# Attention followed by a swish MoE layer on one core: the num matmuls in 64x64 array tiles, one batch loaded earlier, the last rows in two column halves

## The chip, the cores and the metric

The kernel runs on one core of a Trainium2 chip. The time is the device time of one execution in microseconds (us). A profile of one execution per kernel gives the rest. The profile's span leaves out about 2 us of the time (327.5 us of span beside about 329 us).

The engines are called TensorE (PE in the profile, its weight loads PEld), VectorE (DVE), ScalarE (ACT), GpSimd (POOL) and SyncE (SP). "L287" is a line of the kernel that the profile belongs to; the lines of the two kernels differ.

## The reference

```python
# q, k, v: (B=8, H=8, S=576, D=64); w_in: 512x2048; w_out: 2048x512; beta: 2048
phi(x) = concat([relu(x) * cos(theta), relu(x) * sin(theta)], -1)   # theta = pi/2 * pos / S
kv  = einsum('bhsf,bhsd->bhfd', phi(k), v);   z = sum_s phi(k)
num = einsum('bhsf,bhfd->bhsd', phi(q), kv)
den = einsum('bhsf,bhf->bhs',   phi(q), z) + 1e-6
x   = (num / den), heads joined: 4608 tokens x 512
h   = x @ w_in
out = (h * sigmoid(beta * h)) @ w_out
```

The two large products take 9 chunks of 512 tokens with 64 matmuls each into h and into o. Attention is small beside them, but it must be done first for the tokens of a chunk.

## The kernel before

Attention of batch 0 is a prologue; that of batch 1 lies between the matmuls of chunk 0, that of batches 2 to 7 between those of chunks 1 to 6. Chunks 7 and 8 have none. A chunk has 32 slots: 16 groups of four h matmuls, then 16 parts of four o matmuls.

The num matmuls contract over 128 rows: two heads lie above each other, so each head's kv block is padded with zeros beside it, and 2 x 65 columns stream through. (65 is 64 values and the sum for the denominator.)

```python
    kv = one.tile([P, 2, 2, 2, 2 * E], BF16, name="kv")        # E = 65
    nc.gpsimd.memset(kv, 0.0)
    ...
    def num_mm(b, t, jp, bank):
        for i in range(3):
            n = 3 * t + i
            for cs in range(2):                                # cos, sin
                for g in range(2):
                    gs_ = slice(g * HP, (g + 1) * HP)
                    nc.tensor.matmul(
                        ps[gs_, bank, i * 2 * E : (i + 1) * 2 * E],
                        lhsT=(qt, qs)[cs][:, jp, n, gs_],
                        rhs=kv[:, g, jp, cs, :],
                        start=(cs == 0), stop=(cs == 1))
```

Each of batches 2 to 7 has three bursts of 24 such matmuls, in slots 16, 18 and 20 of its chunk. The loads stand in one queue, and w_in 3 is cast on GpSimd:

```python
    load_w("out", 0)
    load_w("out", 1)          # needs a staging buffer that the cast of a w_in tile must free
    load_raw(1, "v")          # so batch 1's v stands behind that wait
    load_raw(1, "k")
    load_raw(1, "q")
    ...                       # cast w_in 2 on VectorE
    load_w("out", 2)
    ...                       # cast w_in 3 on GpSimd
    load_w("out", 3)
    early = {                 # chunk 0: what is put behind which slot
        5: lambda: cast_wout(0),
        8: lambda: cast_wout(1),
        13: lambda: (v_scale(1, 0), [v_scale(1, 1, jp, eng="pool") for jp in range(2)]),
        17: lambda: k_relu(1),
        20: lambda: (kv_mm(1, 0, 6), kv_mm(1, 1, 6), q_relu(1, 0), kv_take((0, 1), 6), q_relu(1, 1)),
        ...                   # q turned at 22 and 23, num at 25, 26 and 28
    }
```

The last 128 rows of the output are one 512-column product in one bank. ScalarE copies its left half, VectorE its right half afterwards.

## Time and profile before

| | before |
|---|---|
| time, median of the runs before the change | 328.77 us (328.76 to 329.08) |
| span of the profiled run | 327.5 us |
| start of the first h matmul (end of the prologue) | 22.15 us |
| chunk 0 | 48.35 us, clock 0.89 |
| each of chunks 1 to 6 | about 32.5 us, clock 1.00 |
| each of chunks 7 and 8 | 28.44 us |
| last matmul's end to the span's end | 5.15 us |

The prediction below shows the views that carry the argument: TensorE's busy row, the table of stretches and the chain of waits. The page of the kernel before has this group (line, engine, operation, operands with partitions x elements, count; then busy us, mean ns of one, and the idle time just before them).

```profile
L289 PE MATMUL ps<-kv,qt 128*64 128x130 bf16 x288 | 20.3, 226 | 0.4 <-ACT kv L279 0.3
```

`128*64` is the part of the array that one matmul uses: all rows, half of the columns. The 226 ns is a latency, not the price of a matmul: 24 of them pass in 0.82 us. The reader should price pipelined matmuls by the distance between starts.

### The profile page before, as it was taken

The numbers are of one execution on the slowest core, as the hardware profiler recorded it, in microseconds if no ns is written. First come the engines' busy times: TensorE is split into PE (matmuls) and PEld (weight loads), VectorE is DVE, ScalarE is ACT, GpSimd is POOL, SyncE is SP. The second block draws the span as 40 slices with busy tenths as digits, with TensorE's granted clock in tenths as the row PEclk, the third lists the DMA queues.
The fourth block names the chain that finished last, engine by engine and source line by source line (L and its number), as shares of the span: only waits on it lengthen the run. The fifth ranks groups of instructions, "written<-read, shape, count | busy, mean of one in ns | idle before, by whom it ended". The sixth has DMA issues, their size and how long they took to land.

```text
span 327.5 us, 5827 instructions
## 1 busy us (share of the span) xinstructions
PE 309.5 (94%) x2410; PEld 147.3 (45%) x2410; DVE 122.3 (37%) x267; ACT 141.3 (43%) x220; POOL 87.2 (27%) x95
## 2 busy tenths in 40 slices
PE   8989927999999999999999999999999999999993
PEld 3554413454554455445444544454445444444441
DVE  4989386381374037403740383038303200000000
ACT  7557405277313731373147314721472147327510
POOL 2556040074025402630263026302720220000000
PEclk9999978799999999999999999999999999999999
DMA  7992999259559706980797079606500620121022
GB/s 251 394 344 97 373 390 392 91 106 318 211 121 274 311 2 127 247 334 3 133 272 303 2 140 297 270 9 141 127 0 10 130 64 1 30 68 32 0 66 64
DMA packets 49530, 53.60 MB, mean 164 GB/s; under 512 B 30288, under 2 KB 30304, under 8 KB 49504
## 3 DMA queue, kind: packets, MB, share of 16 engines
q1 hardware_dynamic: 46784, 45.88, 45.8%
q0 software_dynamic: 2688, 7.34, 8.1%
q8 instruction: 19, 0.31, 0.4%
q14 instruction: 7, 0.06, 0.1%
q10 hardware_dynamic: 32, 0.01, 0.0%
HBM read 36.71 MB, written 9.44 MB: 141 GB/s over the span
## 4 chain that ended last, share of the span: by engine, by line
PE 82%; DMA 9%; DVE 3%; POOL 2%; SPq 1%; ACT 1%; issue 0%; ACTq 0%; DVEq 0%
PE ps L390 38%; PE ps L377 36%; PE ps L289 5%; DMA w_stage<-in_moe_w_in_dram 5%; PE ps L265 3%; DMA raw_v<-in_v_dram 3%; DVE vb L220 2%; POOL win L105 2%; DMA raw_q<-in_q_dram 2%; SPq L95 1%; ACT wout L114 1%; DVE qs L223 1%; DVE rk L197 0%; PE ps L354 0%; ACT o_sb L400 0%
## 5 line engine op out<-in xcount | busy, mean ns | idle before, releaser
L390 PE MATMUL ps<-wout,g_t 128*128 128x512 bf16 x576 | 132.4, 383 | 2.8 <-ACT wout L114 2.8
L377 PE MATMUL ps<-xt,win 128*128 128x512 bf16 x576 | 133.9, 378 | 1.2 <-ACT xt L360 1.2
L381 ACT ACTIVATE g_t<-ps,beta 128x512 bf16<-128x512 f32 x144 | 98.9, 687 | 41.9 <-PE ps L377 41.9
L377 PEld LDWEIGHTS <-win 128*128 128x128 bf16 x576 | 55.2, 97 | 75.8 <-issue 15.4
L390 PEld LDWEIGHTS <-g_t 128*128 128x128 bf16 x576 | 54.8, 98 | 68.8 <-issue 5.9
L404 POOL DMA_DIRECT2D out_dram<-o_sb x56 | 37.7, 678 | 151.9 <-ACT o_sb L400 151.9
L400 ACT COPY o_sb<-ps 128x512 f32<-128x512 f32 x35 | 20.5, 585 | 111.9 <-PE ps L390 111.9
L281 DVE CAST kv<-ps 64x520 bf16<-64x520 f32 x14 | 9.8, 698 | 79.8 <-PE ps L265 79.7
L223 POOL TENSOR_TENSOR qs<-qt,tanr 128x1152 bf16<-128x1152 bf16 x12 | 28.4, 2386 | 5.0 <-PE ps L377 4.9
L398 DVE COPY o_sb<-ps 128x256 f32<-128x256 f32 x1 | 0.4, 425 | 65.5 <-ACT o_sb L397 65.5
L220 DVE TENSOR_SCALAR vb<-raw_v,cos 128x256 bf16<-128x256 f32 x63 | 20.8, 405 | 1.7 <-DMA raw_v<-in_v_dram 1.7
L289 PEld LDWEIGHTS <-qt 128*64 128x64 bf16 x288 | 16.4, 113 | 10.2 <-issue 9.6
L289 PE MATMUL ps<-kv,qt 128*64 128x130 bf16 x288 | 20.3, 226 | 0.4 <-ACT kv L279 0.3
L307 DVE TENSOR_TENSOR xs<-ps,rden 128x768 bf16<-128x768 f32 x21 | 20.1, 957 | 0.7
L289 PE MATMUL ps<-kv,qs 128*64 128x130 bf16 x288 | 19.9, 225 | 0.0
L302 DVE TENSOR_TENSOR den<-ps,eps 128x12 f32<-128x12 f32 x21 | 3.6, 170 | 40.5 <-PE ps L289 40.5
L265 PE MATMUL ps<-vb,rk 64*64 64x130 bf16 x576 | 11.4, 230 | 6.7 <-DVE rk L197 6.5
L289 PEld LDWEIGHTS <-qs 128*64 128x64 bf16 x288 | 16.6, 111 | 0.0
L220 DVE TENSOR_SCALAR vb<-raw_v,sin 128x256 bf16<-128x256 f32 x54 | 14.7, 348 | 0.0
L265 PEld LDWEIGHTS <-rk 64*64 64x64 bf16 x576 | 9.9, 114 | 10.4 <-DVE rk L197 7.0
L210 POOL TENSOR_TENSOR vb<-raw_v,sin 128x1152 bf16<-128x1152 f32 x4 | 8.8, 2213 | 15.9 <-DMA raw_v<-in_v_dram 15.9
L240 ACT COPY qt<-ps 128x640 bf16<-128x640 bf16 (+1 forms) x8 | 4.9, 640 | 18.2 <-PE ps L235 15.8
(57 smaller groups left out, 114.4 us busy)
## 6 DMA issues: line engine op xcount, KB each, us to landing
raw_v<-in_v_dram SPq DMA_DIRECT2D x7, 1152.0 KB, 11.5
raw_k<-in_k_dram SPq DMA_DIRECT2D x7, 1152.0 KB, 13.8
raw_q<-in_q_dram SPq DMA_DIRECT2D x7, 1152.0 KB, 8.8
out_dram<-o_sb POOLq DMA_DIRECT2D x56, 128.0 KB, 4.7
w_stage<-in_moe_w_in_dram SPq DMA_DIRECT2D x4, 1024.0 KB, 15.3
w_stage<-in_moe_w_out_dram SPq DMA_DIRECT2D x4, 1024.0 KB, 11.0
out_dram<-o_sb SPq DMA_DIRECT2D x16, 128.0 KB, 2.3
raw_q<-in_q_dram SPq DMA_DIRECT2D x2, 576.0 KB, 4.6
```

The source lines that it names most:

```text
L210: (nc.gpsimd if eng == "pool" else nc.vector).tensor_tensor(vb[:, n0:n1, js, cs, 0:D], rv.rearrange("q j n d -> q n j d")[:, n0:n1, js], t ...
L220: nc.vector.tensor_scalar(o, a, scalar1=t[:, n : n + 1], scalar2=None, op0=ALU.mult)
L223: eng.tensor_tensor(dst.rearrange("q n (g p) -> q n g p", g=2), src.rearrange("q n (g p) -> q n g p", g=2), tanr[:, n0:n1].unsqueeze(2).to ...
L265: nc.tensor.matmul(t[jj * HP : (jj + 1) * HP, g], lhsT=rk[hs, n, 2 * jp + jj, :], rhs=vb[hs, n, 2 * jp + jj].rearrange("q s e -> q (s e)") ...
L281: nc.vector.tensor_copy(o, a)
L289: nc.tensor.matmul(ps[gs_, bank, i * 2 * E : (i + 1) * 2 * E], lhsT=(qt, qs)[cs][:, jp, n, gs_], rhs=kv[:, g, jp, cs, :], start=(cs == 0), ...
L307: nc.vector.tensor_tensor(xs[:, 3 * t : 3 * t + 3].rearrange("q n s (j d) -> q s n j d", j=2), nv[:, :, :, :, 0:D], rden.unsqueeze(4).to_b ...
L377: nc.tensor.matmul(h_ps, lhsT=win[jt // 4][:, mi, (jt % 4) * P : (jt % 4 + 1) * P], rhs=xt[:, :, jp, g * HP : (g + 1) * HP], start=(mi == ...
L381: nc.scalar.activation(g_t, h_ps, AF.Silu, scale=beta[:, jt : jt + 1])
L390: nc.tensor.matmul(o_ps, lhsT=gs[c, jt][:, tt * P : (tt + 1) * P], rhs=wout[jt // 4][:, jt % 4, :], start=(jt == 0), stop=(jt == JT - 1))
L400: nc.scalar.copy(o_sb, o_ps)
L404: eng.dma_start(out=out_v[bb, n], in_=o_sb[hf * HP : (hf + 1) * HP, :])
```

## The change

Its intent: num uses the four 64x64 tiles of the array at once, so no zeros are multiplied and only 65 columns stream; one burst per batch instead of three costs fewer entries and exits; batch 1's v and k come ahead of w_out, so that chunk 0 doesn't wait for them; the last rows' copy overlaps their own matmuls. The diff, cut to its core:

```diff
-    kv = one.tile([P, 2, 2, 2, 2 * E], BF16, name="kv")
+    kv = one.tile([P, 2, 2, 2, E], BF16, name="kv")
-    nc.gpsimd.memset(kv, 0.0)
@@ v_scale: VectorE reads cos/sin from a PSUM copy
+            if eng == "dve":
+                t = ps[:, 1, 32 + 16 * cs : 32 + 16 * cs + NQ]
@@ num
+    def num_mm(n, jp, bank, slot):
+        for cs in range(2):
+            for jj in range(2):
+                rows = slice(jj * HP, (jj + 1) * HP)
                 for g in range(2):
+                    cols = slice(g * HP, (g + 1) * HP)
                     nc.tensor.matmul(
+                        ps[cols, bank + jj, slot * E : (slot + 1) * E],
+                        lhsT=(qt, qs)[cs][rows, jp, n, cols],
+                        rhs=kv[rows, g, jp, cs, :],
                         start=(cs == 0), stop=(cs == 1))
@@ loads
+    load_raw(1, "v")
+    load_raw(1, "k")
     load_w("out", 0)
     load_w("out", 1)
-    load_raw(1, "v")
-    load_raw(1, "k")
     load_raw(1, "q")
+    load_w("out", 2)
+    load_w("out", 3)
     for gj in GJ:
         cast_win(2, gj)
-    load_w("out", 2)
+    v_scale(1, 0)
     for gj in GJ:
-        cast_win(3, gj, "pool")
-    load_w("out", 3)
+        cast_win(3, gj)
@@ chunk 0 (cut)
+        5: lambda: v_scale(1, 1),
+        7: lambda: cast_wout(0),
+        9: lambda: k_relu(1),
+        11: lambda: cast_wout(1),
+        19: lambda: (kv_mm(1, 0, 6), kv_mm(1, 1, 6), q_relu(1, 0), q_relu(1, 1), kv_take((0, 1), 6),
+                     cast_wout(2, "aaaa")),
@@ batches 2 to 7
-        for t, (slot, bank) in enumerate(((16, 4), (18, 6), (20, 4))):
-            u.append((slot, lambda t=t, bank=bank: (
-                num_mm(b, t, 0, bank), num_mm(b, t, 1, bank + 1), x_div(b, t, bank))))
-            u.append((slot + 1, lambda t=t: x_turn_dma(b, t)))
+        u.append((18, lambda: (num_all(0, 4), num_all(1, 6), num_all(2, 0))))
+        for t, bank in enumerate((4, 6, 0)):
+            u.append((18, lambda t=t, bank=bank: (x_div(t, bank), x_turn_dma(b, t))))
@@ the last 128 rows
+    def o_last(c, tt):
+        o_sb = osb_pool.tile([P, DM], FP32, name="o_sb", tag="o_sb")
         for hf in range(2):
+            m0, m1 = 256 * hf, 256 * hf + 256
+            o_ps = ps[:, 4 + hf, 0:256]
+            ...                                   # 16 matmuls of 256 columns
+            (nc.scalar.copy if hf == 0 else nc.vector.tensor_copy)(o_sb[:, m0:m1], o_ps)
+            store(c, tt, o_sb, m0, m1)
```

The prologue's num and divisions of batch 0 are regrouped to fit (7 + 2 of the nine token groups instead of 3 x 3), and its warm-up matmuls are moved.

## The prediction

> **What bounds the kernel now.** I read four views in this order: the page's clock and busy rows, the chain that ended last in order of time, the same chain at its end, and the table of stretches. First the rows of TensorE in 40 slices of 8.19 us, and its granted clock.
>
> ```profile
> PE   8989927999999999999999999999999999999993
> PEclk9999978799999999999999999999999999999999
> ```
>
> TensorE is full except in slices 5 to 7 (41 to 57 us), and there its clock fell too. That is chunk 0 (a chunk is 512 tokens: 64 matmuls into h, then 64 into o), which runs from 22.15 to 70.50 us. The table of stretches sets it beside chunk 1, chunk 2 and a late chunk that has no attention work (columns: stretch, length, then busy time of PE, PEld, DVE, ACT, POOL, clock, DMA share, GB/s).
>
> ```profile
> 22.15:70.50 48.35, 38.38 (x308) 19.23 (x309) 31.91 (x52) 21.37 (x35) 12.80 (x12) 0.89 0.69 248
> 70.50:103.13 32.63, 32.63 (x273) 15.46 (x273) 17.61 (x47) 13.19 (x20) 11.78 (x11) 1.00 0.80 214
> 103.13:135.61 32.48, 32.48 (x274) 15.36 (x272) 12.79 (x32) 13.33 (x20) 10.26 (x10) 1.00 0.59 174
> 265.50:293.94 28.44, 28.44 (x129) 12.46 (x128) 0.00 (x0) 13.33 (x20) 1.03 (x2) 1.00 0.17 38
> ```
>
> So there are two kinds of loss: 16 us in chunk 0 against a chunk with the same work, and 4.04 us of attention matmuls in each of chunks 1 to 6, where TensorE never waits. The chain says what held chunk 0 (columns: start, length, what).
>
> ```profile
> 25.80 1.24 POOL win L105
> ...
> 31.14 0.37 SPq L93
> 31.51 0.05 issue
> 31.56 8.43 DMA raw_v<-in_v_dram
> 39.99 0.03 issue
> 40.02 6.16 DVE vb L220 x9
> 46.18 1.28 DVE rk L197
> 47.46 0.04 issue
> 47.50 2.17 PE ps L265 x69
> ```
>
> The second w_out load got a staging buffer that a slow cast on POOL held until 31.1 us; batch 1's v stands behind it in the same queue, so it is only issued at 31.56, lands at 39.99, and is scaled at 0.68 us an instruction because POOL works beside it. The kv matmuls wait 6.5 us for that, and the idle halves the clock. In steady state the chain is TensorE alone:
>
> ```profile
> 115.04 1.15 PE ps L265 x72
> 116.18 2.83 PE ps L377 x12
> 119.01 0.86 PE ps L390 x4
> 119.88 0.82 PE ps L289 x24
> 120.70 1.83 PE ps L390 x8
> 122.53 0.82 PE ps L289 x24
> ```
>
> L265 is kv, L289 num, L377 h, L390 o. The end is a copy in two halves, the second waiting for the first:
>
> ```profile
> 322.46 0.38 ACT o_sb L397
> 322.84 0.02 issue
> 322.87 0.42 DVE o_sb L398
> ```
>
> **What the Trainium skill says.** (1) "TensorEngine Tiling (Array Packing)", Key Properties: tiles of the array work in parallel, and a change of tiling mode drains TensorE. The trace agrees: kv, in 64x64 tiles, starts its matmuls in groups of four, one group each 57 ns for 130 columns; and the last o matmul before a num burst starts 0.31 us before the first num matmul instead of 0.216. (2) "TensorE: Matmul & The Clock Gate", LDWEIGHTS: a weight load takes columns/1.2 ns, thus 53 ns for 64 columns, as an estimate. The kernel before cannot confirm it: 57 ns is longer than both 53 ns and the 54 ns of the stream. (3) The same page, What's actually happening: after an idle window of about 3.4 us the clock is halved. The trace agrees: 6.5 us idle, then o matmuls 0.43 us apart instead of 0.216. (4) "SBUF — State Buffer", Who interferes with whom: a VectorE instruction with two SBUF inputs is blocked by a GpSimd one that reads SBUF. The trace agrees: of two equal scalings of v in the prologue, the one under POOL's took 3.08 us, the other, overlapped for 0.72 us, took 1.93 us; both leave about 1.2 us.
>
> **The change, part by part.**
>
> *num in four tiles.* Before, a num matmul contracts 128 rows, half of them zeros, with 130 columns moving, in pairs: per batch 72 matmuls, 36 pairs, three bursts of 0.82 us = 2.46 us. The o matmuls around them take 0.86 + 1.83 + 1.83 + 9.60 = 14.12 us against 13.81 us in a chunk without bursts: 0.31 us for three entries and exits. Together 2.77 us. Check: 32.48 - 28.44 = 4.04 = 2.77 + 1.15 (kv) + 0.11 (kv's entry and exit). After, 144 matmuls of 65 columns, no zeros, in 36 groups of four, one burst. What sets a group's time is open: the stream, 65 columns at 512 per 0.2158 us = 27 ns, plus 3 ns as kv shows, 30 ns; instruction issue: kv's instructions start 1.7 ns apart, eight make 14 ns, so it does not bind; or the weight loads at 53 ns plus 3. I give 30 ns 0.6, something about 43 ns (odd column counts, starts at 260-byte steps) 0.25, and 57 ns 0.15: mean 37 ns. Burst: 36 x 37 ns = 1.33 us, plus one entry and exit 0.2 (a little more than 0.1, for the first load) = 1.5 us. Gain 1.25 us a batch, six batches in chunks 1 to 6: **7.5 us**. Divisions (about 1.36 us each on VectorE) come three in a row after the burst; 12 us of o matmuls remain to hide them, so nothing is added. The kv eviction becomes one instruction instead of two; VectorE has slack there, so it gains nothing by itself.
>
> *Batch 1 ahead of w_out.* In the built order batch 1's v and k stand directly behind the four w_in loads, and the second w_out load now waits for a VectorE cast. Bytes come at about 390 KB/us in order of issue. w_in's last load has 15 of its 16 completions by 23.7 us and the last at 25.75 us, one DMA engine being 2 us late. v (1.18 MB, 3.0 us) then lands at 26.7, the late engine at 28.8 us; k at 29.7 and 31.8; w_out 0 and 1 by about 34 and 37; q by 40. VectorE: the casts of w_in 1 and 2 end about 27; then v scaled with cos, now placed before the cast of w_in 3, waits until 28.8: 9 x 0.26 = 2.4 -> 31.2; w_in 3, 4 x 0.69 -> 34.0. TensorE needs w_in 3 for h groups 12 to 15. The prologue is shorter: v is scaled from a PSUM copy of cos, so 3.08 us becomes about 1.2, and num is smaller, so h can start about 20.2 instead of 22.15 us; group 12 would be due at 20.2 + 12 x 0.914 = 31.2, and waits until 34.0. So the prologue's 2 us are lost to this **new wait** (it was 33.1 for group 12 before). h ends at 37.4. Then VectorE: v with sin 36.4, w_out 0 38.0, k 39.4, w_out 1 41.0, q 42.5, kv eviction 43.2. TensorE reaches kv after four o parts at 37.4 + 3.45 = 40.9: k is ready, the 6.5 us wait is gone, and so is the halved clock (kv 2.17 -> 1.15, nine o matmuls 0.21 us each, part of num: about 3.6 us). ACT: w_out 2 from about 43 to 45.8, q's four copies to 48.8, w_out 3 to 51.2, before the o part that needs it (53.6). Chunk 0's end: 37.4 + o 13.8 + kv 1.25 + two q turns 1.25 + num 1.5 + entries 0.3 + x turns 1.1 + small waits 0.9 + last x copy 0.9 = 58.4 against 70.50: **12.1 us**.
>
> *Last rows in two column halves.* 32 matmuls of 256 columns, 3.49 us by the same column rate plus 3 ns each, instead of 16 x 0.216 = 3.45. The first half is copied and stored under the second; at the end stands one 0.42 us copy instead of 0.38 + 0.42 in a row: **0.4 us**.
>
> Sum: 7.5 + 12.1 + 0.4 = 20.0; 328.8 - 20.0 = 308.8, rounded to 309.
>
> **The rivals.** *Weight loads bind num.* Then groups stay near 57 ns, the burst is 2.05 + 0.2 = 2.25 us, the gain 0.5 us a batch, 3 in all and 0.7 less in chunk 0: 314. For it: the skill's 53 ns. Against it: recorded load lengths, which may be modelled, are 107 ns for 64 columns and 98 ns for the 128-column loads, which come in four chunks of 32; the 9 to 10 ns between them look like 32 columns at the full rate. *The new wait for w_in 3 grows.* A further delay of the late DMA engine by 1.5 us (its lag grew so between 18.4 and 20.4 us, when instructions were fetched over the DMA engines; the program now has more) holds v to 30.3, h to 39, and an idle near 3.4 us may halve the clock once more: chunk 0 ends about 60 to 61, total 311. Taken with the first: 316. *Loads were hidden anyway*: if a later wait (w_out 2 or 3, q) took kv's place, chunk 0 would keep several of the 16 us, but by the order of bytes w_out 3 lands at about 45 us, 8 us early. *All goes well*: v lands at 26.7, no late engine, chunk 0 ends at 56, num at 30 ns: 305.
>
> **Range and chances.** The two large terms are nearly independent: chunk 0 gives 10 to 14 us, num 3 to 9. Ends that take one bad term each give 305 and 314, with both half bad 315; 8 times in 10 I expect 304.5 to 315.5. Faster by over 2% means under 322.2; even num at no gain and chunk 0 at 10 us gives 318. Faster 0.95, within 2% 0.04, slower 0.01 (a stall in the burst or divisions that hold up the next chunk).
>
> **What would show it.** Right: chunks 1 to 6 about 31.2 us long, one num burst of 1.3 to 1.6 us each, 144 matmuls, groups of four 30 to 40 ns apart; kv of batch 1 starting at about 41 us with the clock at 1.0 through chunk 0; a wait of 2 to 3 us before h group 12 released by VectorE's cast of w_in 3, with v landing near 28.8; only VectorE's copy after the last matmul. Wrong: groups at 57 ns; v landing beyond 31 us; a clock of 0.5 in chunk 0; VectorE's divisions on the chain in chunks 1 to 6.

## The result and the profile after

The changed kernel took 308.21 us (307.17 to 310.27, four runs) beside 328.76 us (327.96 to 329.08, four runs) of the kernel before on the same chip. The ratio is 0.9386 with a 95% interval of 0.9331 to 0.9441. A ratio here is the mean time of one kernel's fast runs over the mean of the other's fast runs in the same rounds, so it is not quite the quotient of the medians. The prediction of 309.0 was met. The stages of the two profiles, beside what was predicted:

| stage | before | predicted | after | change, predicted | change, measured |
|---|---|---|---|---|---|
| first h matmul | 22.15 | 20.2 | 22.84 | -2 | +0.7 |
| kv of batch 1 starts | 47.50 | 40.9 | 40.90 | -6.6 | -6.6 |
| end of chunk 0 | 70.50 | 58.4 | 57.01 | -12.1 | -13.5 |
| chunks 1 to 6, each | 32.48 | 31.2 | 31.16 | -1.25 | -1.32 |
| ... all six | | | | -7.5 | -7.9 |
| end of the last matmul to the end of the span | 5.15 | | 4.35 | -0.4 | -0.8 |

The measured changes, with +0.1 for the longer last chunk, add up to -22.1 us, which is the difference of the two spans (327.5 - 305.4). The medians differ by 20.6: the profiled run was the fastest of its four, and the runs' clocks (0.994, 0.994, 0.993, 0.987) explain it only in part: the slowest run has the lowest, but the two runs at 0.994 lie 1.66 us apart. The experiments come back to it.

First TensorE's busy row and its clock on the page of the changed kernel, in slices of 7.64 us:

```profile
PE   7849999999999999999999999999999999999994
PEclk9979999999999999999999999999999999999999
```

The hole at 41 to 57 us is gone. There is a smaller one in the third slice, with a lower clock: in the prologue, where the kernel before had none so deep. The table of stretches of the changed kernel (stretch, length, busy time of PE, PEld, DVE, ACT, POOL, clock, DMA share, GB/s) for chunk 0, chunk 2 and chunk 7:

```profile
22.84:57.01 34.17, 32.98 (x379) 16.88 (x383) 29.30 (x66) 22.63 (x37) 3.18 (x5) 1.00 0.94 335
...
88.33:119.48 31.15, 30.89 (x342) 14.66 (x344) 11.91 (x31) 13.34 (x20) 10.48 (x10) 1.00 0.65 186
...
244.12:272.56 28.44, 28.34 (x128) 12.46 (x128) 0.00 (x0) 13.34 (x20) 1.04 (x2) 1.00 0.17 38
```

Chunk 0 fell from 48.35 to 34.17 us, at clock 1.00, with the DMA busy 94% of it. Chunk 2 fell from 32.48 to 31.15, and chunk 7, which the change leaves alone, kept its 28.44. The chain of waits of the changed kernel, from batch 0's second num burst to batch 1's kv (start, length, what):

```profile
15.09 0.38 PE ps L287 x29
15.46 2.59 issue
18.05 0.59 PE ps L287 x38
...
21.78 1.02 ACT xt L351
...
22.84 1.02 PE ps L368 x4
...
40.90 1.15 PE ps L266 x72
```

L266 is kv, L287 num, L368 h, L386 o. kv of batch 1 comes without a wait and at full clock: 1.15 us instead of 2.17. But TensorE stops for 2.59 us in the middle of a num burst, and the profile says "issue", that is, it sees nothing that it waits for. In steady state, the chain of waits of chunk 2:

```profile
104.25 2.54 PE ps L386 x11
106.79 1.36 PE ps L287 x130
108.15 0.16 issue
108.31 1.89 PE ps L386 x8
```

One burst of 1.36 us stands where three of 0.82 us were. (It has 144 matmuls; the profile lost some records.) The page's group of these matmuls shows the new shape, and puts that one stop of 2.6 us beside them:

```profile
L287 PE MATMUL ps<-kv,qs 64*64 64x65 bf16 x576 | 11.5, 194 | 2.6 <-issue 2.6
```

In chunk 2 the weight loads of successive groups of four start 28 to 36 ns apart, with two longer distances of 54 and 59 ns: 33 ns is the median, 34 ns the mean. (The expectations below say 33.6.) And the end of the chain:

```profile
297.55 3.51 PE ps L402 x32
...
301.14 0.42 DVE o_sb L405
```

One copy stands alone behind the last matmul, as intended.

### The profile page after: what moved, and what is told of

The parts are those of the page before. It is cut to its first block, busy times and chain, and to the rows that moved or that the text cites. A ratio compares the mean times of both kernels' runs of the same rounds, so it can differ in the third digit from the quotient of the medians.

```text
span 305.4 us, 6998 instructions
## 1 busy us (share of the span) xinstructions
PE 291.2 (95%) x2973; PEld 140.5 (46%) x3001; DVE 111.5 (37%) x275; ACT 141.3 (46%) x218; POOL 77.6 (25%) x88
## 4 chain that ended last, share of the span: by engine, by line
PE 91%; DVE 3%; issue 2%; DMA 2%; ACT 1%; SPq 0%; DVEq 0%
PE ps L368 43%; PE ps L386 39%; PE ps L287 3%; PE ps L266 3%; DMA raw_q<-in_q_dram 2%; PE ps L402 1%; DVE qs L224 1%; PE ps L346 1%; DVE vb L211 1%; PE ps L411 1%; ACT xt L351 0%; PE ps L236 0%; DVE xs L309 0%; DVE rk L196 0%; ACT o_sb L392 0%
## 5 line engine op out<-in xcount | busy, mean ns | idle before, releaser
L368 PE MATMUL ps<-xt,win 128*128 128x512 bf16 x576 | 134.0, 378 | 1.7 <-ACT xt L351 1.7
L386 PE MATMUL ps<-wout,g_t 128*128 128x512 bf16 x535 | 120.5, 379 | 2.2 <-issue 1.3
L368 PEld LDWEIGHTS <-win 128*128 128x128 bf16 x576 | 55.2, 97 | 76.1 <-issue 16.6
L386 PEld LDWEIGHTS <-g_t 128*128 128x128 bf16 x560 | 53.9, 98 | 63.5
L278 DVE CAST kv<-ps 128x520 bf16<-128x520 f32 x7 | 4.9, 700 | 80.1 <-PE ps L266 80.1
L309 DVE TENSOR_TENSOR xs<-ps,rden 128x768 bf16<-128x768 f32 (+4 forms) x25 | 22.7, 912 | 0.8
L298 DVE TENSOR_TENSOR den<-ps,eps 128x12 f32<-128x12 f32 (+2 forms) x24 | 3.9, 161 | 36.5 <-PE ps L287 36.5
L287 PE MATMUL ps<-kv,qs 64*64 64x65 bf16 x576 | 11.5, 194 | 2.6 <-issue 2.6
L287 PEld LDWEIGHTS <-qt 64*64 64x64 bf16 x576 | 10.5, 106 | 4.5 <-issue 3.8
L287 PE MATMUL ps<-kv,qt 64*64 64x65 bf16 x576 | 11.6, 195 | 0.3 <-ACT kv L276 0.2
L287 PEld LDWEIGHTS <-qs 64*64 64x64 bf16 x576 | 10.5, 105 | 2.7 <-issue 2.7
L196 DVE TENSOR_SCALAR qb<-raw_q 128x1152 bf16<-128x1152 f32 x15 | 10.7, 752 | 1.5 <-DMA raw_q<-in_q_dram 1.5
L266 PE MATMUL ps<-vb,rk 64*64 64x130 bf16 x576 | 10.2, 218 | 0.7 <-DVE vb L211 0.4
L266 PEld LDWEIGHTS <-rk 64*64 64x64 bf16 x576 | 8.6, 106 | 4.4 <-issue 3.5
L196 DVE TENSOR_SCALAR rk<-raw_k 128x2304 bf16<-128x2304 f32 (+1 forms) x8 | 10.2, 1277 | 0.0
```

The lines of the kernel that those rows point to most:

```text
L196: nc.vector.tensor_scalar(dst, src, scalar1=0.0, scalar2=None, op0=ALU.max)
L266: nc.tensor.matmul(t[jj * HP : (jj + 1) * HP, g], lhsT=rk[hs, n, 2 * jp + jj, :], rhs=vb[hs, n, 2 * jp + jj].rearrange("q s e -> q (s e)") ...
L278: nc.vector.tensor_copy(o, a)
L287: nc.tensor.matmul(ps[cols, bank + jj, slot * E : (slot + 1) * E], lhsT=(qt, qs)[cs][rows, jp, n, cols], rhs=kv[rows, g, jp, cs, :], start ...
L309: nc.vector.tensor_tensor(o.rearrange("q j n s d -> q j (n s) d"), nv[:, :, a:z, :, 0:D].rearrange("q j n s d -> q j (n s) d"), rden[:, :, ...
L368: nc.tensor.matmul(h_ps, lhsT=win[jt // 4][:, mi, (jt % 4) * P : (jt % 4 + 1) * P], rhs=xt[:, :, jp, g * HP : (g + 1) * HP], start=(mi == ...
```

## The experiments

Twelve runs went to the chip: eleven new kernels and, as e11, the changed kernel once more. The first four take the change apart. All gave correct results.

### e1: only num in four tiles, three bursts, on the old kernel

Batches 1 to 7 of the kernel before get the new num tiles, reading the diagonal blocks of the old padded kv; loads and everything else stay.

```diff
+                            nc.tensor.matmul(
+                                ps[cols, bank + jj, (2 * i + jp) * E : (2 * i + jp + 1) * E],
+                                lhsT=(qt, qs)[cs][rows, jp, 3 * t + i, cols],
+                                rhs=kv[rows, g, jp, cs, jj * E : (jj + 1) * E],
+                                start=(cs == 0), stop=(cs == 1))
@@
-                num_mm(b, t, 0, bank), num_mm(b, t, 1, bank + 1), x_div(b, t, bank))))
+                num4(t, bank), x_div4(t, bank))))
```

> The kernel before, with only the num matmuls of batches 1 to 7 in four 64x64 tiles (three bursts a batch as before, loads, prologue and tail as before). Theory (the tiles themselves save the time): groups of four about 33.6 ns apart as in the changed kernel, a burst 12 x 0.034 + 0.2 to 0.25 = 0.6 to 0.65 us instead of 0.92, so about 0.9 us a batch in chunks 1 to 6 (32.48 to about 31.6 us), 5.4 us there and about 1 us in chunk 0: 322 to 323 us in all. Rival (what pays is merging three bursts into one): hardly any gain, over 326 us.

Measured: 321.40 us (321.12 to 323.05, four runs), ratio 0.9807 (0.9778 to 0.9836); the kernel before took 328.38 in this job. Chunks 1 to 6 took 31.54 us, as expected. Each of the three bursts took 0.51 us in the chain of waits, instead of 0.82; the first of them in chunk 2:

```profile
116.76 0.51 PE ps L303 x48
```

So the tiles alone are worth 7.0 us by the medians (the interval lies clear of 1, but reaches over a gain of 2%, so by that measure the verdict is unclear), and the weight-load rival, with 57 ns a group, is out.

### e2: only the loads and their order

The kernel before gets the new order of loads, casts and early slots of chunk 0; num stays as it was.

```diff
+    load_raw(1, "v")
+    load_raw(1, "k")
     load_w("out", 0)
     load_w("out", 1)
-    load_raw(1, "v")
-    load_raw(1, "k")
@@
-        cast_win(3, gj, "pool")
+        cast_win(3, gj)           # and v_scale(1, 0) ahead of it; slots 5 to 23 as in the change
```

> The kernel before, with only the order of loads, the engine and order of the casts and the slots of batch 1 in chunk 0 taken from the changed kernel; num, prologue and tail as before. Theory: kv of batch 1 starts at about 40 us and the clock stays at 1.0; h starts at 22.15 us as before, v lands near 27.3 us, no wait for the cast of w_in 3; chunk 0 ends about 57.8 us instead of 70.5; total about 316 us. Rival (part of chunk 0's gain came from the shorter prologue or from num): chunk 0 ends beyond 60 us, total over 318 us.

Measured: 316.52 us (315.79 to 316.87, four runs), ratio 0.9643 (0.9620 to 0.9667), clock 0.997 to 0.999. h starts at 22.58, chunk 0 ends at 57.54 instead of 70.50; chunks 1 to 6 keep 32.47. The chain of waits of e2 has no wait before kv (L265; h is L377), which takes 1.15 us as at full clock:

```profile
22.58 14.49 PE ps L377 x64
...
40.52 1.15 PE ps L265 x72
```

So the order of loads is worth 11.9 us by the medians. With e1's 7.0, the end's 0.8 (e4) and the 2.3 for one burst instead of three (e3) the parts sum to 22.0, against 20.6 for the whole change by the medians and 22.1 between the two profiled runs. As the four runs of the changed kernel lie 3.1 us apart, this is rough agreement and no more. Note that e2's chunk 0 ends within 0.6 us of the changed kernel's, though it has the old num: the changed kernel's chunk 0 is shorter by 0.8 us (34.17 against 34.96), but its h starts 0.26 us later.

### e3: the changed kernel with three bursts

```diff
-        u.append((18, lambda: (num_all(0, 4), num_all(1, 6), num_all(2, 0))))
-        for t, bank in enumerate((4, 6, 0)):
-            u.append((18, lambda t=t, bank=bank: (x_div(t, bank), x_turn_dma(b, t))))
+        for t, (slot, bank) in enumerate(((16, 4), (18, 6), (20, 4))):
+            u.append((slot, lambda t=t, bank=bank: (num_all(t, bank), x_div(t, bank))))
+            u.append((slot + 1, lambda t=t: x_turn_dma(b, t)))
```

> The changed kernel, with num of batches 2 to 7 again in three bursts at the old slots, on the old banks. Theory (each entry into and exit from the tile mode costs about 0.2 to 0.25 us): chunks 1 to 6 grow from 31.16 to about 31.6 us, 2.5 to 3 us in all, 311 us. Rival (the number of bursts does not matter, the matmuls do): within 0.5 us of the changed kernel, 308 us.

Measured: 312.37 us (310.81 to 313.57, four runs), ratio 0.9519 (0.9476 to 0.9561). Chunks 1 to 6 take 31.55 us, 0.39 more than in the changed kernel, 2.3 us in all. (By the medians e3 is 4.2 us longer. Its profiled run starts h 0.7 us later than that of the changed kernel; the rest of the difference is not seen in a profile.) The chain of waits of chunk 2 of e3 shows where it is:

```profile
106.15 0.51 PE ps L287 x45
106.66 0.16 issue
106.82 1.67 PE ps L386 x7
108.49 0.51 PE ps L287 x41
```

Three times 0.51 + 0.16 is 2.01 us, against 1.36 + 0.16 = 1.52 for the one burst; part of the difference is given back in the o matmuls around them. Two more entries and exits thus cost 0.39 us, 0.2 each, which is the price that the prediction set.

### e4: the changed kernel with the old end

```diff
-        nc.scalar.copy(o_sb, o_ps)
+        if c == NTC - 1 and tt == TT - 1:
+            nc.scalar.copy(o_sb[:, 0:256], o_ps[:, 0:256])
+            nc.vector.tensor_copy(o_sb[:, 256:], o_ps[:, 256:])
+        else:
+            nc.scalar.copy(o_sb, o_ps)
@@
-            elif c == NTC - 1 and slot >= 28:
-                if slot == 28:
-                    o_last(c, 3)
```

> The changed kernel with the last rows as before: one bank of 512 columns, its halves copied by ACT, then VectorE. In the trace of the changed kernel 4.3 us lie between the last matmul's end and the end of the span, before 5.15 us, and the 32 narrow matmuls take 0.09 us more than 16 wide ones. Theory: the stretch after the last matmul goes back to 5.1 us, so the total is 0.7 to 0.8 us longer, which one round can not show against the spread of the changed kernel; the trace decides. My prediction's figure was 0.4 us.

Measured: 310.56 us (309.80 and 311.31, two runs), ratio 0.9466 (0.9431 to 0.9501); such a small part can't be read from the time. From the last matmul to the end of the span it is 5.17 us, against 4.35. The chain of waits at the end of e4:

```profile
302.58 0.38 ACT o_sb L393
...
302.98 0.42 DVE o_sb L394
```

So the new end is worth 0.8 us: 0.4 from the copy, as predicted, and 0.4 that the prediction didn't count. In the changed kernel the last store lands 2.6 us after its copy, in the kernel before 2.9 us; its rows are half as wide. That makes 0.3 of the second 0.4; the rest is not accounted for.

### The stop of TensorE

The stop of 2.59 us in the prologue was not predicted. In e3 and e4, with the same prologue, it is there again, so it is no accident. From the last start before it to the first after it, it lasts 2.78 us in the changed kernel, 3.20 in e3 and 3.50 in e4; lengths below are measured so. The trace has one clue. On the page, one DMA queue is of the kind "instruction": 23 transfers with 0.38 MB, 16 KB each, in the changed kernel, and 19 in the kernel before. If one such block holds 256 instructions, 23 blocks are 5888 and 19 are 4864; TensorE has 2973 + 3001 = 5974 and 2410 + 2410 = 4820. So this queue seems to feed TensorE. I then counted TensorE's instructions in program order, weight loads and matmuls together, and looked where the stop falls: between the 437th and the 439th in all three. (This numbering, which the expectations use too, runs seven short of the trace: there 444 weight loads and matmuls start before the stop in e5, e8, e9 and e11, and 442 in these three, where two matmul records are missing. Shifts and distances are the same in both counts.) The theory: TensorE stands at the end of a block and the next one has not come, because its transfer queues behind the loads. The rival: the stop belongs to the num burst, its PSUM banks or the tiles. Extra warm-up matmuls at the start of the prologue tell them apart: they shift the block's end to another matmul.

### e5: 40 more TensorE instructions ahead of the stop

```diff
-    warm_pe(7)
+    warm_pe(6)
+    warm_pe(21, w=24)
```

> The changed kernel with one wide warm-up matmul at the start replaced by 21 of 24 columns: 40 more TensorE instructions ahead of everything, no other change. In the changed kernel TensorE stops for 2.6 us inside batch 0's second num burst, and instructions are fetched in that time. Theory A (TensorE runs out of instructions; the stop is tied to a place in the instruction stream, program index 437): the stop comes at the same index, thus 40 instructions earlier in the work (20 matmuls earlier in the num burst), and is shorter by about 1 us, as the fetch is asked for earlier: 1 to 2 us. Theory B (the stop is a dependency of that matmul): it stays before the same matmul and keeps its 2.6 us.

Measured: 310.03 us (307.99 to 310.65, four runs), ratio 0.9448 (0.9411 to 0.9485). The stop falls between the 437th and 439th instruction again, which is now a different matmul, 40 instructions earlier in the work. That speaks for the theory. Its length, 2.57 us against 2.78, was expected to fall by about 1 us: a miss.

### e6: 150 more

```diff
-    warm_pe(7)
+    warm_pe(82, w=44)
```

> The changed kernel with the 7 wide warm-up matmuls at the start replaced by 82 of 44 columns: 150 more TensorE instructions ahead. Theory A (instructions): the fetch is asked for some 5 us earlier, no stop over 1 us within batch 0's num; h starts about 20.3 us instead of 22.84, if the narrow warm-up itself does not delay the prologue. Then h group 12 is due about 31.4 us, before VectorE's last cast of w_in 3 ends at about 32.7, and the wait that I predicted appears, 1 to 1.5 us; chunk 0 ends about 55.8 us instead of 57.0; total about 307 us. Theory B (a dependency): the stop stays, total 308 us or more.

Measured: 306.86 us (305.90 to 309.04, four runs), ratio 0.9372 (0.9330 to 0.9413). No stop at 437; the block was read at 10.17 us, long before. A new, shorter one falls between 693 and 695, before batch 0's transposes (L346), where there is no num matmul at all. From e6's view of what TensorE waited for, between 8 and 30 us (line, releaser, us in total, times, longest):

```profile
PE ps L346 <- issue: 1.5, 1, 1.5
```

693 - 437 is 256, the block's size. The rival, num or its banks, can't make this stop. The wait before h group 12 for w_in 3's cast, expected if h starts earlier, was not seen: h started only at 22.33, and group 12 at 35.59 without it. Chunk 0 ended at 58.85 in the profiled run, the slowest of the four, and not at 55.8 as expected: a miss, though the total came out as expected.

### e7: e6, with v's scaling behind the cast of w_in 3

```diff
-    v_scale(1, 0)
     for gj in GJ:
         cast_win(3, gj)
+    v_scale(1, 0)
```

> The kernel of the 150 additional instructions, and v's scaling with cos moved behind VectorE's cast of w_in 3. If the wait for w_in 3 is real there, it vanishes here: h runs without a gap, chunk 0 ends about 55 us; the waits for q's turned copies behind ACT's scaling of w_out 2 may take back up to 1 us. Total about 306 us. If h group 12 was not held by that cast, no difference from the kernel without this move.

Measured: 308.47 us (306.25 to 309.40, four runs), ratio 0.9403 (0.9353 to 0.9454). The stop at 693 came again, h started at 22.0 and chunk 0 ended at 57.77. As there was no wait in e6 that this could remove, it tells nothing of it: a miss, and inconclusive.

### e8: extra num-like bursts of other widths

Chunks 2 to 5 each get one more burst of 144 matmuls in the same tiles, results unread, with 65, 33, 17 and 130 columns.

```diff
+            if slot == 24 and c in (2, 3, 4, 5):
+                probe({2: 65, 3: 33, 4: 17, 5: 130}[c])
```

> The changed kernel with an additional burst of 144 matmuls in four 64x64 tiles, with the same loads of 64 columns and results that nobody reads, in chunks 2, 3, 4 and 5, with 65, 33, 17 and 130 moving columns. Theory of the prediction (stream sets the pace, about 3 ns besides): 31 to 34, 17, 10 and 57 ns from group to group. Rival (a floor from weight loads or issue): 33 and 17 columns stay at one floor, 27 ns if 64 columns are loaded at one a cycle of the full clock, 53 ns excluded already by the 33.6 ns of the changed kernel.

Measured (one run, 318.9 us, state unknown; only lengths inside its trace are used). From the start of the burst's first matmul to that of its last:

| columns | 17 | 33 | 65 | 130 |
|---|---|---|---|---|
| burst, us | 1.327 | 1.570 | 1.475 | 2.027 |
| the same by 36 groups of four, ns | 37 | 44 | 41 | 56 |

A quarter of the columns saves 4 ns of 41, and twice the columns cost 15 ns, where their stream alone would cost 27 ns (65 columns at 512 per 0.2158 us). So in this probe the stream does not set the pace at 65 columns and below. The means hide how regular it is. By the starts of the weight loads in the trace, the median distance from group to group is 33 ns at 17, at 33 and at 65 columns, and 56 ns at 130. The differences between the means come from single longer distances: every fourth group of the later part takes about 59 ns at all widths, and there is one of 152 ns at 65 columns and two of 124 and 171 ns at 33. Num's own median is the same 33 ns. So num's pace is best read as the same floor, which a quarter of the columns does not lower in the probe, and not as its stream. Whether the weight loads or the issue of eight instructions make this floor, and where the longer distances come from (the probe writes the same columns of two banks again and again, num goes through six banks), stays open. The stop in the prologue came again at 437, 3.85 us long.

### e9, e10, e11: the stop avoided, or not, beside the changed kernel, five rounds on one chip

e9 has 120 more TensorE instructions early on, e10 the same and e7's exchange, e11 is the changed kernel once more.

```diff
-    warm_pe(7)
+    warm_pe(67, w=54)             # e9 and e10
@@ e10 only
-    v_scale(1, 0)
     for gj in GJ:
         cast_win(3, gj)
+    v_scale(1, 0)
```

> The changed kernel with 67 warm-up matmuls of 54 columns at the start in place of 7 of 512: 120 more TensorE instructions ahead. In the runs so far TensorE stops at program index 437 or 693, 256 apart, whenever it gets there within about 6 us of passing the index 256 before it. Theory A (two blocks of 256 instructions are held, the next is fetched when one is used up): here index 437 is the start of batch 0's second kv half and 693 lies behind h's first matmuls, so neither comes within 6 us of the one before: no stop over 0.7 us in batch 0's num or x turns; h starts about 20.5 to 21.5 us, the clock stays at 1.0. h group 12 is then due before VectorE's last cast of w_in 3 (about 32.7 to 33.7 us) and waits up to 1.3 us. Total 306 to 307 us, 1.5 to 2 us under the changed kernel of the same job. Theory B (the stops have other causes): a stop of about 2 us remains somewhere before h.

> The same with v's scaling with cos behind the cast of w_in 3. If h group 12 waited in the run before, it does not here, and the total is 1 us less, 305 to 306 us; if it did not wait there, the two are equal.

> The changed kernel once more, unaltered, as the measure for the two others on the same chip: 308 us, with a spread of 1 to 1.5 us from run to run that comes from the prologue (the stop at index 437 and the half clock after it), as its chunks 1 to 8 take the same time in each trace.

Measured, six runs each, beside 327.44 us of the kernel before:

| | median (range) | ratio (95%) | stop in the profiled run | h starts | chunk 0 ends |
|---|---|---|---|---|---|
| e11 | 310.15 (308.12 to 310.65) | 0.9463 (0.9431 to 0.9495) | at 437, 3.12 us | 23.5 | 59.77 |
| e9 | 307.10 (305.95 to 309.89) | 0.9391 (0.9352 to 0.9429) | at 437, 2.92 us | 23.4 | 57.56 |
| e10 | 306.90 (305.99 to 308.34) | 0.9382 (0.9349 to 0.9414) | none | 20.20 | 56.41 |

The shift alone is worth 2.4 us by the means (307.41 of e9 against 309.76 of e11), shift and exchange together 2.7 (307.03 of e10); neither interval touches e11's. e9's profiled run still stopped, at the same index, now inside kv, which theory A had excluded: its block was read only at 14.61 us, e10's at 11.03, though both had the same instructions before. So the shift gives the block more time but doesn't make it safe. In e10's profiled run h starts at 20.20, which is what the prediction gave for a prologue without a stop. But its chunk 0 then takes 36.21 us, against 34.17 in the changed kernel: of the 2.64 us by which h starts earlier only 0.60 are left at the end of chunk 0, and other waits take the rest (e12 looks at one). In e11's profiled run chunk 0 takes 36.29 us, its first part at half clock. e9's six clocks run from 0.988 to 1.0; the three runs at 0.998 and above took 305.95 to 306.72, the others 307.49 to 309.89.

The traces give this table (e1 and some blocks without a stop are left out). It was worked out from the records of the instruction transfers and TensorE's instructions, and is no view of the profile: when TensorE reached the last instruction of a block, when the read of the next block began, and when TensorE went on (us).

```
run      block end   reached   read began   went on   went on - read began
after       437       15.27      15.57       18.05      2.48
e3          437       15.48      16.16       18.68      2.52
e4          437       16.19      17.32       19.69      2.37
e5          437       16.40      16.37       18.97      2.60
e8          437       16.16      17.41       20.01      2.60
e9          437       14.19      14.61       17.11      2.50
e11         437       15.94      16.56       19.06      2.50
e6          693       18.57      17.93       20.30      2.37
e7          693       18.58      17.88       20.27      2.39
e6          437       14.07      10.17       no stop
e10         437       14.74      11.03       no stop
e12         437       14.94      11.31       no stop
e10         693       21.17      17.80       no stop
before      437       23.66      18.03       no stop
e2          437       24.09      19.08       no stop
```

In every case with a stop TensorE goes on 2.4 to 2.6 us after the read of the next block began, whatever it was doing. In every case of the table without one the read began 3.3 us or more before the block's end was reached; later in the kernels blocks are read as little as 2.5 us ahead, without a stop. I take this as shown for the cause of the stop: it follows the index through four different shifts and the read through nine cases. What is not shown is what sets the moment of the read. The traces show it beside another moment, that at which TensorE passes the instruction 256 places ahead of the block's end: the read began 3.4 us after it in the kernel before and 3.6 us after it in the changed kernel, thus at nearly the same distance. But the kernel before took 8.8 us for those 256 instructions and the changed kernel 3.3 us. In e10 the distance was 3.0 us, in e12 1.8, and in e9, alike up to there, 6.2; in the prologue the 16 DMA engines are 90% busy and more with the loads, but that this is the reason is not shown.

The kernel before reached its 437th instruction only in chunk 0 at 23.66 us, when the block had long come. Num in four tiles has twice as many instructions; that is how the change brought the stop into the prologue. The clock was halved after it: at 18.4 to 21.8 us in the changed kernel, 21.2 to 28 us in e11, and not at all between 13 and 30 us in e10's profiled run.

e10 and e9 don't differ within their intervals, so the exchange of v's scaling and w_in 3's cast is worth nothing that can be seen.

### e12: e10, with two of w_out 2's scalings moved

e10's chain of waits in chunk 0 names a new one: ScalarE scales w_out 2, only then copies q, and num waits.

```profile
43.63 1.32 ACT wout L114 x2
44.95 0.58 ACT qt L241
...
45.56 2.16 DVE qs L224 x3
...
47.77 0.52 PE ps L287 x35
```

```diff
-                     cast_wout(2, "aaaa")),
+                     cast_wout(2, "ddaa")),          # two of four on VectorE
```

> Edit: e10_shift120_cast with two of the four scalings of the third w_out tile moved from ScalarE to VectorE. In e10's profile ScalarE scales that tile from 42.39 us (it landed at 42.37) for 2.56 us before it copies batch 1's q, and num of batch 1 starts only at 47.77. Theory: these copies are what num waits for in chunk 0 once the stop of TensorE is gone; with half of the scaling on VectorE, which stands idle at 41.7 to 42.4, the q copies come about 1.3 us earlier, num starts near 46.7, chunk 0 ends near 55.5 instead of 56.4, and the mean is about 306 us against 307 of e10 (0.934 of the kernel before). Rival: another wait takes its place (the division before the second burst, or the last x tile), and the time stays at e10's 0.938 within 0.003. If TensorE stops again for instructions in the profiled run, the profile can't tell and only the runs' ratio counts.

Measured, on another chip: 305.60 us (305.08 to 307.85, six runs), mean 306.20, ratio 0.9349 (0.9313 to 0.9385), with 327.48 us for the kernel before. The profile has no stop. The wait is gone from the chain; num follows the o matmuls directly:

```profile
43.96 2.59 PE ps L386 x12
46.55 0.55 PE ps L287 x47
```

num starts at 46.55 (expected 46.7) and chunk 0 ends at 55.23 (expected 55.5), though h, which started at 20.40, had to wait 0.56 us for the cast of w_in 0 in this run (0.18 in e10's). Part of the rival holds too: the chain still has VectorE's division between the two num bursts. The ratio is 0.0033 below e10's, the size expected, but the two intervals overlap and the chips differ, so the time alone doesn't show the gain; the trace does. This is the fastest kernel here: 0.4% or 1.2% less than the changed kernel, by the ratios 0.9349 and 0.9386 or 0.9463.

## Why the prediction was right, and where not

**The bound and the two kinds of loss: right.** Chunk 0 and the attention matmuls of chunks 1 to 6 gave 21.4 of 22.1 us. e2 and e1 show each by itself: e2 leaves chunks 1 to 6 at 32.47 us, and of e1's 7.0 us 5.6 lie there, the rest being batch 1's num in chunk 0 and spread. (In the prediction's row of slices, counted from 0, only 5 and 6 have the hole; in slice 7, at 57 to 66 us, only the clock is low.)

**num: the size right, the reason given most weight not.** The gain was 1.32 us a chunk against 1.25. Of the three candidates for a group's time (30, 43, 57 ns) the first, at 0.6, was the stream. The chip gave 33 ns at the median and 34 in the mean, near that candidate but, by e8, not for its reason: the probe shows the same 33 ns at 17 columns, where the stream would be 7 ns by the same column rate. That the floor lies so close above the stream's 30 ns is luck. The burst came to 1.36 + 0.16 = 1.52 us, predicted 1.5. The prediction also set issue aside by kv's starts 1.7 ns apart; e8 doesn't bear that out or refute it. The entry and exit at 0.2 us were right (e3: 0.39 for two). The rival, weight loads at 53 ns, fell. The divisions stayed hidden.

**Chunk 0: right to 1.4 us, for two errors that cancel.** The step that failed is "h can start about 20.2 instead of 22.15 us; group 12 would be due at 20.2 + 12 x 0.914 = 31.2, and waits until 34.0". h started at 22.84, because TensorE stopped 2.59 us for its next block of instructions and ran at half clock after it. And the new wait before group 12 didn't come: v landed at 27.31 instead of 28.8 (14 of its 16 completions came by 25.99, and the last 1.3 us later instead of 2.1), the cast of w_in 3 ended at 32.72, and group 12 began at 33.68 without a gap. Predicted were a start 2 us earlier and a loss of 2.8; found were a start 0.7 later and no loss. kv then started at 40.90, predicted 40.9, which looks exact and isn't. Whether the wait would have come without the stop stays open. By an estimate from these figures it would: group 12 due at 31.2 and the cast done at 32.72 leave 1.5 us. But no profiled run with v's scaling ahead of the cast had h at 20.2, and e9's runs that look free of the stop are as fast as e10's.

**The fetch of instructions: seen, at the wrong place.** The prediction names it among the rivals, as something that might delay a load's late DMA engine by 1.5 us. It delayed TensorE itself. The first number of that step was right without it: e10, which had no stop, started h at 20.20. But that start brought chunk 0's end forward by only 0.60 us: from kv's start (38.92) to the end e10 takes 17.5 us, the changed kernel 16.1.

**The rest of chunk 0.** From kv's start at 40.90 to its end it took 16.1 us, predicted 17.5: the allowances for small waits and turns were 1.4 too much.

**The end: mechanism right, size off.** 0.4 predicted, 0.8 measured; the shorter landing of half-width rows was not in the sum.

**Range.** 308.2 lies inside, and so does e11, 310.15 on another chip. The two profiled runs differ by 2.76 us (307.17 and 309.93), and so do their ends of chunk 0 (57.01 and 59.77): that difference is the longer stop and half clock, neither of which the range was made for.

## What to carry to other kernels

Read a small matmul's price from the distance between starts, and test whether fewer columns would still bring something: in the probe here groups of four started 33 ns apart at 17 columns as at 65, while each entry into other tiles and back cost 0.2 us. Put loads in the order in which they are first needed, and look for a load that stands behind one that waits for a buffer; here that was worth 12 of 20.6 us. When a change adds instructions to a prologue full of transfers, count them: "issue" before a matmul in the middle of a burst can be an instruction block that has not come, and more warm-up matmuls ahead of it can move it out of the way, as in e10 and e12, though e9 shows that they need not.

## What the Trainium skill lacked or had wrong

- "TensorE: Matmul & The Clock Gate", LDWEIGHTS (loading the stationary operand): it gives columns/1.2 ns, so 53 ns for 64 columns. Four loads into four tiles and their four matmuls passed every 33 ns here (median), so the figure can't be used as a price per group in tiles.
- The same page, Wait — 56ns, not 53.3ns?: it says that matmuls never start less than about 25 ns apart. In four 64x64 tiles 144 matmuls started in about 1.2 us, 8.4 ns each, so the figure can hold only for the starts in one tile; there the floor was 33 ns (median) at 17, 33 and 65 columns in e8.
- "Runtime: NRT & Kernel Launch", Instruction fetch mechanics: blocks of 16 KiB and 256 instructions agree with the trace (stops at 437 and 693). It calls the cost of crossing into the next block mostly hidden; in steady state no stop was seen here, but with the DMA engines filled by loads TensorE stood still 1.7 to 3.9 us, until 2.4 to 2.6 us after the block's read began.
- "TensorEngine Tiling (Array Packing)", Key Properties: a change of mode drains TensorE, without a price. Here an entry and exit cost about 0.2 us (e3).
